# Filter loads of a spectral-mixer kernel: five ahead of the first weight transpose, four from GpSimd, the rest one to a row step

## Chip, cores and metric

The kernel runs on one core of a Trainium2 chip. The metric is the device time of one execution in microseconds; the median of several executions is compared. A core has five instruction streams that matter here: TensorE (PE in the profile, with its weight loads as PEld), VectorE (DVE), ScalarE (ACT), GpSimd (POOL) and SyncE (SP). SP computes nothing: it issues DMAs, in the order in which the program lists them, and an SP instruction that has to wait holds up all SP instructions after it. GpSimd can issue DMAs as well; they are a separate queue in the profile (q0, software_dynamic), while those of SP are q1 (hardware_dynamic).

## What is computed

The reference is the forward pass and all gradients of two residual blocks on x of 2048 x 448 in bf16:

```python
def _A_ref(x, w_r, w_i):
    X = rfft2(x.astype(float32)); X = X * (w_r + 1j * w_i)
    return irfft2(X, s=(S, D)).astype(bfloat16)
def _B_ref(x, w1, b1, w2, b2):
    h = _layernorm(x); u = gelu(einsum("bsd,sf->bdf", h, w1) + b1)
    return transpose(einsum("bdf,fs->bds", u, w2) + b2)
h  = x + _A_ref(_layernorm(x), w_r, w_i)
h2 = h + _B_ref(_layernorm(h), w1, b1, w2, b2)
# outputs: h2 and the gradients of sum(h2 * grad_out) by x, w_r, w_i, w1, b1, w2, b2
```

w_r and w_i, the spectral filter, are 2048 x 225 each. They are the tensors whose loads the change moves. w2 is 1792 x 2048.

## The kernel before, in words

The Fourier transforms are matrix products with tables that the kernel generates itself. The 2048 rows are 128 partitions times NT = 16 steps t. All four engine orders of PE, SP, DVE and ACT are written out by hand: an engine runs its instructions in the order of the Python program. GpSimd alone is ordered by a planner at build time. The part that matters here is the first 50 us of the run:

* **Start.** SP loads x, grad_out and four natural blocks of w2 (j = 0 to 3), which PE transposes itself (`turn_w2`). The other ten blocks of w2 (j = 4 to 13) come by transposing DMAs on SP, `load_w2T`, line 312. Five buffers go round: three in the region rE, two in rO.
* **Row steps** (`for t in range(NT)`, line 903). A step has a first product `row_a(t + 1)` for the next row group, with the folded input (`folds`, region rS, made on DVE by `fold_prep` or `fold_quarters`, one for two row groups) as stationary side and a scaled table `Rs[t + 1]` (region rX, `scale_R`, DVE) as moving side; then a second product `row_b(t - 3)`. Between them PE is filled with products of another matrix, w2 by grad_out (`dg_gen`, pulled by `fill(n)`). `scale_R(t + 3)` needs `rstd_x`, the inverse deviation of the layer norm. It is computed by Newton steps on GpSimd for two row groups at a time (`newton_gp`, lines 408 to 414), at the steps listed in `GROUPS`; the last group, rows 14 and 15, comes at t = 7.
* **Reshape.** When `row_b` has done two row groups and the result has left PSUM, a DMA on SP (line 687) lays it out for the next stage in D2. There are eight such DMAs; each is 226 KB.
* **Filter loads.** `w_io` (line 577) is a generator of 18 loads into rW: nine for w_r, nine for w_i. In each nine, numbers 0, 2, 4, 6 take 16 x 3600 elements (16 partitions), numbers 1, 3, 5, 7 take 16 x 16 x 225 (15 for number 1) in reversed order of rows, and number 8 takes 16 x 225. All are issued on SP. `W_AT` tells how many are drawn in step t: two in even steps and one in odd steps, t = 0 to 11.
* **Spectral stage** (`s2_stage`, line 690). It begins with products of 32 x 32 tables with D2 (lines 709 and 225, tile r as moving side), needs all of D2, and then multiplies by the filter on DVE (`fwd_mult`), which needs rW.

The first transposing DMA is issued at the head of step 0:

```python
    W_AT = {t: 1 if t % 2 else 2 for t in range(12)}
    for t in range(NT):
        if t == 0:
            load_w2T()
```

Of the kernel before, what the change touches and what calls it, by code (L numbers as in the profile page):

```python
# [103 lines left out]
class Ring:  # L104
# [7 lines left out]
    def next(self):  # L112
        v = self.views[self.i % len(self.views)]
        self.i += 1
        Ring.release(v)
        return v
# [8 lines left out]
def kernel(  # L125
# [20 lines left out]
    nc = tc.nc  # L146
# [4 lines left out]
    gp_ = nc.gpsimd  # L151
# [12 lines left out]
    def cut(reg, off, *dims):  # L164
        n = int(np.prod(dims))
        v = reg[:, off:off + n]
        if len(dims) == 1:
            return v
        names = "abcd"[:len(dims)]
        return v.rearrange("p (" + " ".join(names) + ") -> p " + " ".join(names),  # L170
                           **{c: d for c, d in zip(names, dims)})
# [131 lines left out]
    def load_w2T():  # L303
        j = w2T_ring.i
        if j == NFB:
            return
        wT = w2T_ring.next()
        w2Ts[j] = wT
        if j < N_NAT:
            nc.sync.dma_start(out=w2n[j], in_=B_w2[j * P:(j + 1) * P, :].rearrange("f (t c) -> f t c", c=P))  # L310
            return
        nc.sync.dma_start_transpose(out=wT, in_=B_w2[j * P:(j + 1) * P, :].rearrange("f (t c) -> f t c", c=P))
# [261 lines left out]
    Wc = cut(rW, 0, 2, NG, DF)  # L574
    W = Wc.rearrange("p c g k -> p g c k")

    def w_io(dr, di, store):
        Wq = Wc.rearrange("(q s) c g k -> s q c g k", s=2)
        for c_, d in ((0, dr), (1, di)):
            moves = []  # L580
            for i in range(4):
                moves.append((Wq[0][16 * i:16 * i + 16, c_].rearrange("l g k -> l (g k)"), 16 * i, [[P * DF, 16], [1, 16 * DF]]))
                g0 = 0 if i else 1
                moves.append((Wq[1][16 * i:16 * i + 16, c_, g0:NG, :], P - 16 * i - g0,
                              [[P * DF, 16], [-DF, NG - g0], [1, DF]]))
            moves.append((Wq[1][0:16, c_, 0, :], 64, [[P * DF, 16], [1, DF]]))
            for sb, row, dims in moves:
                d_ap = bass.AP(d.tensor, d.offset + row * DF, dims)
                nc.sync.dma_start(out=d_ap if store else sb, in_=sb if store else d_ap)
                yield  # L590

    r452_ring = ring(r452, 0, 8, 2, KW)
    Xs = cut(rX, 0, NG, 2, KW)
# [20 lines left out]
    def scale_R(t):  # L614
        v = Rs_ring.next()
        ve.tensor_scalar(out=v, in0=Rm[:], scalar1=rstd_x[:, t:t + 1], scalar2=None, op0=ALU.mult)
        return v
# [5 lines left out]
    def fold_prep(src, t2):  # L623
        ft = fold_ring.next()
        s0 = 2 * t2
        fv = ft[:, 0:2 * D].rearrange("p (s w j) -> p s w j", s=2, w=2)
        a = src[:, s0:s0 + 2, 0:D // 2]
        r = src[:, s0:s0 + 2, D - 1:D // 2 - 1:-1]
        ve.tensor_tensor(out=fv[:, :, 0, :], in0=a, in1=r, op=ALU.add)
        ve.tensor_tensor(out=fv[:, :, 1, :], in0=a, in1=r, op=ALU.subtract)  # L630
        folds[t2] = ft
# [5 lines left out]
    def fold_quarters(src, t2, i=None):  # L637
        ft = fold_ring.next()
        s0 = 2 * t2
        if i is None:  # L640
            i = m448.i % 8
            assert i % 2 == 0
            m448.next(), m448.next()
        pm = cut(r448, i * D, 2, 2, D // 2)
        fv = ft[:, 0:2 * D].rearrange("p (s k j) -> p s k j", s=2, k=4)
        a, b = src[:, s0:s0 + 2, 0:D // 2], src[:, s0:s0 + 2, D // 2:D]
        ve.tensor_tensor(out=pm[:, :, 0, :], in0=a, in1=b, op=ALU.add)
        ve.tensor_tensor(out=pm[:, :, 1, :], in0=a, in1=b, op=ALU.subtract)
        lo, hi = pm[:, :, :, 0:DC], pm[:, :, :, 2 * DC - 1:DC - 1:-1]
        ve.tensor_tensor(out=fv[:, :, 0:4:3, :], in0=lo, in1=hi, op=ALU.add)  # L650
        ve.tensor_tensor(out=fv[:, :, 2:0:-1, :], in0=lo, in1=hi, op=ALU.subtract)
        folds[t2] = ft

    def row_a(t, R):
        pa = ps_ff()
        ft = folds[t // 2]
        for k in range(4):
            o = DC * (4 * (t % 2) + k)
            mm(pa[:, k * P:(k + 1) * P], lhsT=ft[:, o:o + P], rhs=R, start=True, stop=True)
        if t % 4 == 0:  # L660
            blks[t // 4] = blk_ring.next()
        evac(out=blks[t // 4][:, :, t % 4, :], in_=pa[:].rearrange("p (n x) -> p n x", x=8))

    def row_b(h, quarters=None):
        u, e, c = h // 4, h // 2 % 2, h % 2
        if h < 0 or h >= NT:
            return
        pd = ps_ff()
        pv = pd[:, 0:452].rearrange("p (c k) -> p c k", c=2)
        pq = pd[:, 0:452].rearrange("p (c e k) -> p c e k", c=2, e=2)  # L670
        for w in (1, 0):
            for b in range(2):
                n = 4 * (4 * (2 * w + b) + 2 * c + e)
                lhsT = blks[u][0:DC, n:n + 4].rearrange("p i j x -> p (i j x)")
                if quarters is not None:
                    mm(pq[:, 1 - w, b, :], lhsT=lhsT, rhs=quarters[0:DC, w, b, 0:KW // 2], start=True, stop=True)
                    continue
                mm(pv[:, 1 - w, :], lhsT=lhsT, rhs=csF[0:DC, w, b, :], start=(b == 0), stop=(b == 1))
        if c == 0:
            css[h // 2] = cs_ring.next()  # L680
        cs = css[h // 2]
        if quarters is not None:
            evac(out=cs[:, c].rearrange("p w (j e) -> p w e j", e=2), in_=pq)
        else:
            evac(out=cs[:, c], in_=pv)
        if c:
            defer(RESH_LAG, lambda: resh[0].dma_start(out=D2[u:u + 125:4, 8 * e:8 * e + 8].rearrange("p g c k -> p (g c k)"),
                                                      in_=cs.rearrange("p x c k -> p (x c k)")), cs)
# [96 lines left out]
    def fill(n):  # L785
        while n > 0 and pending:
            try:
                next(pending[0])
                n -= 1
                if row_ops:  # L790
                    row_ops.pop(0)()
            except StopIteration:
                pending.pop(0)
# [5 lines left out]
    def ln_stats(src, t, mv):  # L799
        ve.bn_stats(out=stats[:, t, :], in_=src[:, t, :])  # L800
        if t % 2:
            ve.bn_aggr(out=mv[:, t - 1, :], in_=stats[:, t - 1, :])
        if t % 2:
            ve.bn_aggr(out=mv[:, t, :], in_=stats[:, t, :])
# [88 lines left out]
    GROUPS = {0: (6, 8), 1: (8, 10), 3: (10, 12), 5: (12, 14), 7: (14, 16)}  # L893
    STATS = {0: (6, 7), 1: (8, 9), **{t: (t + 8,) for t in range(2, 8)}}
    INV_S = {10: 0, 11: 1, 12: 2, 13: 3}
    W_AT = {t: 1 if t % 2 else 2 for t in range(12)}
    for c in range(2):
        for e in range(2):
            sc.copy(out=Rp.rearrange("p (e a q b c) -> p c e a q b", e=2, c=2, q=8, a=2)[:, c, e],
                    in_=Rm[:, 64 * c + 32 * e:64 * c + 32 * e + 32].rearrange("p (q a b) -> p a q b", q=8, a=2))  # L900
    FILL_A = (4, 4, 8, 12, 6, 3, 3, 3, 3, 3, 3, 3, 3, 3, 3, 3)
    FILL_B = (0, 0, 2, 2, 2, 2, 4, 4, 3, 2, 2, 2, 2, 2, 2, 2)
    for t in range(NT):
        if t == 0:
            load_w2T()
        if t + 1 < NT:
            row_a(t + 1, Rs.pop(t + 1))
        fill(FILL_A[t])
        if 1 <= t and t + 3 < NT:
            if t + 3 in (4, 8, 12):  # L910
                while Meter.side:
                    Meter.side.pop(0)()
            Rs[t + 3] = scale_R(t + 3)
        row_b(t - 3, csQ if t - 3 >= 4 * U_Q else None)
        if t == NT - 1:
            for i in range(t - 2, NT):
                row_b(i, csQ)
        if t % 2 and t < 12:
            if t // 2 + 2 < 2 * U_Q:
                fold_prep(xn, t // 2 + 2)  # L920
            else:
                fold_quarters(xn, t // 2 + 2, t // 2 % 2 * 2)
        if t == 4:
            for w in range(2):
                gp_.tensor_copy(out=csQ[:, w, :, :], in_=csF[:, w, 0, :].rearrange("p (j e) -> p e j", e=2))
        if t == 1:
            sc.activation(out=warm, in_=half_r, func=ACT.Sin, scale=1.0 / 64.0)
            while cs_ops:
                cs_ops.pop(0)()
        for i in STATS.get(t, ()):  # L930
            ln_stats(xn, i, mvx)
        for _ in range(3 if t > 0 else 0):
            if next(uv, None):
                break
        if t in GROUPS:
            a, b = GROUPS[t]
            newton_gp(mvx[:, a:b, 1], rstd_x[:, a:b], slice(a, b))
        for _ in range(W_AT.get(t, 0)):
            next(w_loads, None)
        if t in INV_S:  # L940
            gen_inv_s(INV_S[t])
        if t == 2:
            gen_RT()
        fill(FILL_B[t])
# [500 lines left out]
```

## Time and profile before

| what | value |
|---|---|
| median of 3 runs | 342.64 us (342.21 to 345.09) |
| the profiled execution, its own time | 343.32 us |
| its span, first to last instruction | 341.5 us |
| PE busy | 330.4 us, 97% |
| DVE, ACT, POOL busy | 251.5, 205.2, 82.8 us |
| granted TensorE clock | 1.000 |
| DMA, share of 16 engines: q1 (SP) and q0 (POOL) | 86.7% and 4.9% |

Times in the views are microseconds from the start of the span. Each line of a timeline gives start, duration, engine, line of the code, operation, out<-in, shape, number of instructions merged, and in brackets the idle time of the engine before it with what ended it. A "q" after the engine's name (SPq) marks an instruction that is issued but keeps no arithmetic busy; the duration of an SP DMA is the time to issue it, and the time until its data has landed is listed apart. Tiles without a name of their own are shown as r.

### The profile page before, as it was taken

To read this page: it belongs to the slowest core of one execution; us is meant where nothing else is said; L and a number is where in the kernel's file an instruction comes from. 1 tells how busy PE (TensorE), PEld (TensorE's weight loads), DVE (VectorE), ACT (ScalarE), POOL (GpSimd) and SP (SyncE) were. 2 spreads that over 40 slices of the span, in tenths; PEclk is the share of its full clock that TensorE was granted. 3 is DMA by queue.
4 is the path that set the end of the run, shared out by engine and by line. 5 is a ranking of instruction groups with operands and counts; after the bars stand their busy time and mean duration, and the time that the engine had idled before them with its cause. 6 is when DMAs were issued, how large, how long until landed. Compare 5 with 4: busy or idle time off the path is not lost.

```text
span 341.5 us, 7952 instructions
## 1 busy us (share of the span) xinstructions
PE 330.4 (97%) x2877; PEld 173.5 (51%) x2877; DVE 251.5 (74%) x672; ACT 205.2 (60%) x447; POOL 82.8 (24%) x253
## 2 busy tenths in 40 slices
PE   8899979999999999999999999999999999999995
PEld 4565644456645555555555555554333334555552
DVE  8999438834967888594225988787589984499994
ACT  5886746856966553513222345566478875688882
POOL 7756102451320000001001111120002222156650
PEclk9999999999999999999999999999999999999999
DMA  7998999977999999967976999848998999999975
GB/s 271 396 157 179 194 247 165 198 153 228 252 286 326 330 321 236 222 200 226 207 169 144 177 180 190 159 110 169 236 302 256 232 238 314 273 193 298 230 272 206
DMA packets 137966, 78.03 MB, mean 228 GB/s; under 512 B 88712, under 2 KB 129416, under 8 KB 137800
## 3 DMA queue, kind: packets, MB, share of 16 engines
q1 hardware_dynamic: 135368, 73.82, 86.7%
q0 software_dynamic: 2560, 3.72, 4.9%
q8 instruction: 22, 0.36, 0.5%
q14 instruction: 16, 0.13, 0.1%
HBM read 27.81 MB, written 22.04 MB: 146 GB/s over the span
## 4 chain that ended last, share of the span: by engine, by line
PE 71%; DVE 1%; ACT 1%; issue 0%
PE ps_mm L220 63%; PE ps_ff L220 6%; PE ps_ff L225 2%; ACT rO L84 1%; DVE rA L84 1%; DVE rB L84 0%; ACT rAT L84 0%; ACT rC L84 0%; DVE rG L84 0%; ACT rstd_h L84 0%; DVE rstd_h L84 0%
## 5 line engine op out<-in xcount | busy, mean ns | idle before, releaser
L220 PEld LDWEIGHTS <-r 128*128 128x128 bf16 (+2 forms) x628 | 58.6, 105 | 47.2 <-issue 2.5
L220 PEld LDWEIGHTS <-rS 128*128 128x128 bf16 (+1 forms) x468 | 36.3, 97 | 32.9 <-issue 6.4
L84 ACT CAST rO<-ps_mm 128x512 bf16<-128x512 f32 (+1 forms) x69 | 36.8, 584 | 14.4 <-PE ps_mm L220 13.0
L220 PE MATMUL ps_mm<-rD,r 128*128 128x448 bf16 x224 | 44.5, 352 | 0.0
L220 PEld LDWEIGHTS <-rst 128*128 128x128 bf16 (+1 forms) x320 | 23.6, 97 | 31.3 <-issue 14.0
L724 POOL DMA_DIRECT2D r<-r x32 | 19.2, 606 | 68.8 <-ACT r L84 61.6
L220 PE MATMUL ps_mm<-rC,rE 128*128 128x448 bf16 x144 | 32.1, 353 | 0.6 <-issue 0.6
L220 PE MATMUL ps_mm<-rB,r 128*128 128x448 bf16 x160 | 31.2, 353 | 0.1
L220 PE MATMUL ps_mm<-rG,rst 128*128 128x512 bf16 (+1 forms) x128 | 28.7, 380 | 0.2 <-ACT rO L84 0.2
L220 PE MATMUL ps_mm<-r,rst 128*128 128x512 bf16 (+2 forms) x144 | 27.4, 345 | 0.0
L84 ACT CAST r<-ps_ff 128x452 bf16<-128x452 f32 x44 | 23.7, 587 | 5.8 <-PE ps_ff L225 3.8
L84 ACT ACTIVATE r<-ps_mm,rstd_h 128x448 bf16<-128x448 f32 x16 | 10.1, 634 | 26.8 <-PE ps_mm L220 26.8
L84 DVE SCALAR_TENSOR_TENSOR r<-ps_mm,b2col,r 128x448 bf16<-128x448 f32 x16 | 10.9, 683 | 19.9 <-PE ps_mm L220 18.2
L84 ACT ACTIVATE r<-rC 128x448 bf16<-128x448 bf16 x16 | 9.1, 571 | 26.7 <-DMA out_dram<-r 22.4
L1182 POOL TENSOR_SCALAR lcol<-lcol 128x1 f32<-128x1 f32 x16 | 8.5, 530 | 64.7 <-ACT r L84 64.7
L84 ACT ACTIVATE rG<-rG 128x896 bf16<-128x896 bf16 x14 | 13.3, 950 | 14.9 <-DVE rG L84 14.7
L220 PEld LDWEIGHTS <-rO 128*128 128x128 bf16 (+1 forms) x165 | 15.4, 98 | 12.3 <-ACT rO L84 0.2
L84 ACT CAST rS<-ps_ff 128x512 bf16<-128x512 f32 x32 | 18.7, 589 | 2.5 <-PE ps_ff L220 2.4
L220 PE MATMUL ps_ff<-csI,rAT 113*128 113x224 bf16 (+1 forms) x108 | 19.0, 298 | 0.6 <-ACT rAT L84 0.4
L84 DVE TENSOR_SCALAR rG<-rG 128x896 bf16<-128x896 bf16 x28 | 10.9, 389 | 10.0 <-ACT rG L84 10.0
L220 PE MATMUL ps_mm<-rC,rO 128*128 128x448 bf16 x80 | 18.1, 353 | 0.0
L84 ACT CAST rG<-ps_mm 128x512 bf16<-128x512 f32 (+1 forms) x28 | 13.8, 534 | 6.8 <-PE ps_mm L220 6.7
(199 smaller groups left out, 633.8 us busy)
## 6 DMA issues: line engine op xcount, KB each, us to landing
out_dram<-rO SPq DMA_DIRECT2D x34, 256.0 KB, 2.8
r<-in_B_w_dram SPq DMA_DIRECT2D x5, 1024.0 KB, 8.9
r<-r POOLq DMA_DIRECT2D x32, 113.0 KB, 5.7
out_dram<-rG SPq DMA_DIRECT2D x11, 256.0 KB, 2.3
r<-r SPq DMA_DIRECT2D x12, 226.0 KB, 3.3
r<-in_B_w_dram SPq DMA_DIRECT2D x3, 896.0 KB, 5.4
rS<-in_B_w_dram SPq DMA_DIRECT2D x3, 896.0 KB, 5.8
rB<-in_B_w_dram SPq DMA_DIRECT2D x4, 512.0 KB, 7.6
```

The lines of the kernel that those rows point to most:

```text
L84: fn(**kw)
L220: nc.tensor.matmul(out, lhsT=lhsT, rhs=rhs, start=start, stop=stop)
L225: nc.tensor.matmul(out, lhsT=lhsT, rhs=rhs, start=start, stop=stop)
L724: defer(RESH_LAG, lambda g=g, ab=ab: gp_.dma_start(out=D3[rowbase(g):rowbase(g) + 29:4, :, :, :], in_=ab), ab)
L1182: gp_.tensor_scalar(out=m1, in0=ms, scalar1=-1.0 / D, scalar2=None, op0=ALU.mult)
```

## The change

Three things change in the schedule of the 18 filter loads and of the first transposing load. First, `W_AT` becomes 3 in step 0, 2 in step 1, one each in steps 2 to 5 and 8 to 12, and the first `load_w2T()` moves from the head of step 0 to step 1, behind the loads of that step. Second, of the nine loads of w_i, numbers 0, 2, 4 and 6 are issued by GpSimd, and they are not counted as a draw: number 0 is issued with number 1, and so on. Third, before the first load of w_i a memset on DVE writes one element per partition of rW's w_i half.

```diff
             moves.append((Wq[1][0:16, c_, 0, :], 64, [[P * DF, 16], [1, DF]]))
-            for sb, row, dims in moves:
+            if not store and c_:
+                nc.vector.memset(Wc[:, 1, 0, 0:1], 0.0)
+            for n, (sb, row, dims) in enumerate(moves):
                 d_ap = bass.AP(d.tensor, d.offset + row * DF, dims)
-                nc.sync.dma_start(out=d_ap if store else sb, in_=sb if store else d_ap)
-                yield
+                eng = gp_ if not store and c_ and n in (0, 2, 4, 6) else nc.sync
+                eng.dma_start(out=d_ap if store else sb, in_=sb if store else d_ap)
+                if eng is nc.sync:
+                    yield
...
-    W_AT = {t: 1 if t % 2 else 2 for t in range(12)}
+    W_AT = {0: 3, 1: 2, **{t: 1 for t in (2, 3, 4, 5, 8, 9, 10, 11, 12)}}
...
     for t in range(NT):
-        if t == 0:
-            load_w2T()
         if t + 1 < NT:
             row_a(t + 1, Rs.pop(t + 1))
...
         for _ in range(W_AT.get(t, 0)):
             next(w_loads, None)
+        if t == 1:
+            load_w2T()
```

In the built program the orders of PE and ACT are the same as before. DVE has one instruction more, the memset, between `scale_R(11)` and `scale_R(12)`; the build gives it a wait for four of the w_r loads, those of the numbers 1, 3, 5 and 7. SP has four DMAs fewer. The planner puts the four DMAs of GpSimd one after the other into the Newton steps of row groups 14 and 15, behind line 409 and ahead of the first instruction of line 411; the first of them waits for DVE's memset.

## The prediction

> **What bounds the kernel now.** I read the engine table first, then PE's waits, then the timelines of SP, PE, POOL and DVE over the first 50 us.
>
> ```profile
> PE 330.4 (97%) x2877; PEld 173.5 (51%) x2877; DVE 251.5 (74%) x672; ACT 205.2 (60%) x447; POOL 82.8 (24%) x253
> ```
>
> PE is busy 330.4 of 341.5 us. A change that leaves PE's instructions as they are can win only a piece of PE's 11 idle us. PE's waits, longest first:
>
> ```profile
> PE ps_ff L225 <- DMA r<-rX: 2.4, 1, 2.4
> PE ps_ff L220 <- DVE rS L84: 1.3, 2, 0.7
> PE ps_mm L375 <- DVE rS L621: 1.2, 1, 1.2
> ```
>
> One wait is larger than the others: 2.4 us, once, at the start of the spectral stage, for a reshape DMA out of rX. PE's timeline has the place, and SP's timeline what is ahead of that DMA:
>
> ```profile
> 50.03 0.77 PE L225 MATMUL ps_ff<-r,Vt 32*32 32x452 bf16 x16 [2.37 <-DMA r<-rX]
> ```
>
> ```profile
> 13.59 5.80 SPq L312 DMA_TRANSPOSE rO<-in_B_w_dram  x1
> 19.44 3.31 SPq L589 DMA_DIRECT2D rW<-in_A_w_r_dram  x5
> 22.86 5.56 SPq L312 DMA_TRANSPOSE rE<-in_B_w_dram  x2
> 28.48 1.93 SPq L589 DMA_DIRECT2D rW<-in_A_w_r_dram  x3
> ...
> 42.86 1.91 SPq L589 DMA_DIRECT2D rW<-in_A_w_i_dram  x3
> 44.88 0.58 SPq L687 DMA_DIRECT2D r<-r  x1
> 45.50 0.60 SPq L589 DMA_DIRECT2D rW<-in_A_w_i_dram  x1
> 46.20 2.57 SPq L687 DMA_DIRECT2D r<-rX  x4
> ```
>
> From 13.59 to 48.77 each SP instruction begins within 0.1 us of the end of the one before it: SP does nothing but issue. The last four reshapes go out from 46.20, though the last of their data left PSUM at 43.9 (ACT, rX). So SP's issue time sets the end here, and PE, ready at 50.03 - 2.37 = 47.66, waits for it.
>
> **What goes from SP.** Four loads of w_i leave SP ahead of the last reshape. Three take 1.91 and one has to wait its turn, so 0.64 us each: 4 x 0.64 = 2.6 us. The last reshape would land at 50.03 - 2.6 = 47.4, before PE comes at 47.66. The gain, by this alone, is the whole stall: 2.37 us. What is late next is PE itself.
>
> **Five loads ahead of the first transpose.** The transpose is moved past five loads on SP. SP holds eight DMAs in flight here: each waits for the eighth before it. The transpose had the place of 13.59; the five loads now wait for the start-up loads one by one. By the landings of those start-up loads (4096- and 3584-byte rows, issued at 8.62 and 9.38, landed 18.3 and 19.6) the fifth goes out between 18.4 and 19.6, and the transpose between 19.0 and 20.2. It took 5.80 when it stood in the full queue, and 2.10 to 3.33 later, so I take 2.8: SP is through with the six at 21.8 to 23.0, against 22.75 before. I take 0.6 us ahead, bounds 1.5 ahead and 3.3 behind (20.2 + 5.80). The transposed block (j = 4) is first used by PE at 29.6; the transpose at 13.59 landed after 7.7 us, so at the latest 27.9. It costs nothing, covered by 1.7 us; without that cover PE would wait by the difference.
>
> **The memset.** It is one DVE instruction of about 0.06 us (the memset at 0.80 is that short), but it waits for w_r loads 1, 3, 5 and 7. Load 7 is the 26th SP instruction, as before, when it went out at 29.79 and landed 4.5 us later, at 34.3. With SP 0.6 ahead: 33.7. DVE comes to it at 32.3 (after the first of the two rX at 32.09). So DVE stands for 1.4 us. Behind it on DVE are `scale_R(12)`, the fold for row groups 12 and 13, and `scale_R(13)`; PE waits for that fold with `row_a(12)` at 34.77. The fold ended at 33.82, a slack of 0.9, so PE would stand 0.5 us here. It does not add to the next item, which sets a later time for the same PE order.
>
> **The four DMAs on GpSimd.** This is the item that decides. They stand in the middle of the Newton steps for rows 14 and 15:
>
> ```profile
> 33.74 0.19 POOL L409 TENSOR_SCALAR rstd_x<-mvx 128x2 int32<-128x2 int32 x1
> 34.02 0.19 POOL L411 TENSOR_TENSOR nt_f<-rstd_x 128x2 f32<-128x2 f32 x1
> ...
> 35.95 0.19 POOL L414 TENSOR_TENSOR rstd_x<-nt_f,rstd_x 128x2 f32<-128x2 f32 x1
> ...
> 58.00 2.63 POOL L724 DMA_DIRECT2D r<-r  x4 [14.29 <-ACT r L84]
> 63.04 2.36 POOL L724 DMA_DIRECT2D r<-r  x4 [2.42 <-ACT r L84]
> ```
>
> ```profile
> 36.18 0.32 DVE L84 TENSOR_SCALAR rX<-Rm,rstd_x 128x128 bf16<-128x128 bf16 x1 [0.17 <-POOL rstd_x L414]
> 36.40 0.68 DVE L84 TENSOR_TENSOR r<-rA 128x448 bf16<-128x448 bf16 x2
> 37.12 0.69 DVE L84 TENSOR_TENSOR rS<-r 128x448 bf16<-128x448 bf16 x2
> ...
> 38.33 0.39 PE L220 MATMUL ps_ff<-rX,rS 128*128 128x128 bf16 x4
> ```
>
> The chain: Newton ends 36.14, DVE already waits for it (0.17), scales the table for row 14 at 36.18, folds rows 14 and 15 until 37.81, and PE takes the fold in `row_a(14)` at 38.33. From DVE's end to a waiting PE it takes 0.06 elsewhere (27.14 to 27.20), so the slack is 38.33 - 37.81 - 0.06 = 0.46 us. Four issues on POOL cost 2.63 after a long pause, 2.36 otherwise. The trace has none with rows of 7200 bytes on POOL. From below I bound an issue by a small POOL operation, 0.23 (L984 at 81.40), 0.9 for four; from above by 2.63, and by the longest POOL row here, 0.91, for each of four, 3.6. I take 2.63, the row that is nearest. PE then stands at `row_a(14)` for 2.63 - 0.46 = 2.17 us, if the memset is done when POOL arrives at 33.93 (33.7, so just).
>
> The DVE instructions of those 2.6 us run beside the DMAs or wait for Newton. POOL's issues at 58.00 took 0.60 to 0.84 each with DVE at 900-element products. The Trainium skill (SBUF — State Buffer, the box on DVE blocking DMA in its part on the doors to the memory) says that a GpSimd DMA of some 620 ns takes some 3100 ns beside a DVE copy that locks the shared port. By that page four would be an estimated 12.4 us and PE's stall 11.9. The trace shows no case of it, and DVE is idle in most of that window.
>
> **The sum.** PE comes to the spectral stage at 47.66 + 2.17 = 49.83. The last rows leave PSUM 2.17 later, at 46.0, their reshape needs 2.4 to land: 48.4, so no wait remains. The stage starts at 49.83 instead of 50.03: 0.2 us won. From there PE is gapless but for 0.6, 0.4 and two 0.2 us in the next 40 us, so the shift is carried to the end. The profiled span would be 341.3 and its own time 343.1; that execution stood 0.7 over the median, so the forecast for the median is 342.64 - 0.2 = 342.4 us. In short: the stall of 2.37 at the stage's head is exchanged for one of 2.17 twelve us earlier.
>
> **Rivals.**
>
> *POOL's issue is cheap.* 16 rows of 7200 bytes may cost less than a line-724 DMA (2560 packets of q0 by 32 issues: 80 each). At 0.9 for four, PE stands 0.44 and the stage starts at 48.1, which the reshape (47.4) allows: 1.9 won, 340.7. With the whole stall gone 340.3. For it: the rows are a fifth of that. Against it: SP pays 0.6 for 16 rows and for 240 alike, and POOL's 0.60 is the same in 15 of 16 issues at 58 to 75 us.
>
> *The memset holds everything (slower).* If load 7 lands later than 34.1, POOL's first DMA starts with it, and each us later is a us later at `row_a(14)`. At 34.1 the change is worth nothing; at 35.6 it loses 1.5: 344.1; with the transpose at its old 5.80, load 7 lands at 37.6: 3.5 lost, 346.1. For it: load 7 landed at 34.3 before, already over that point, and three transposes now stand close together ahead of it, each 512 KB. Against it: the first transpose meets an emptier queue.
>
> *SP isn't freed.* Two transposes with only one reshape between them could take back what the four loads gave (2.10 and 3.33 now): the reshape then lands at 50 and PE waits again, 342.9.
>
> *POOL's issue is dear.* At 0.91 each PE stands 3.2 at `row_a(14)`: 343.4. For it: the first issue at 58.00 took 0.84. Against it: none of the others did.
>
> **How the numbers follow.** Forecast 342.4 (341.8 to 343.0): 0.46. Cheap POOL issue (340.3 to 341.8): 0.25. Late memset (343.0 to 346.1): 0.19. SP not freed: 0.05. Dear POOL issue: 0.05. The range, 340.3 to 344.8, leaves out the end of the late memset (0.07), of the dear issue (0.03) and a little below. One per cent, 3.4 us, is about what this measurement can tell from nothing. Faster by more needs more than the whole stall: 0.03. Slower by more is the end of the late memset, 0.05, and an issue dearer than any row, 0.02. Within: 0.90.
>
> **What would show it.** PE's wait for the DMA from rX should be gone or under 0.3 us. A new PE wait of about 2.2 us should stand at a `ps_ff` product of rX and rS, ended by DVE rS, near 38 to 41 us. POOL should show four DMAs of rW at 34 us, and Newton's last line 414 at 38.8. The memset on DVE should start between 32.3 and 34.8, released by a DMA. SP should begin its last four reshapes when their data is there, not when it is free. Wrong would be: no stall at `row_a(14)` (then POOL's issue is cheap), or the stage's head still waiting for SP.

## The result and the profile after

The changed kernel is slower: 349.15 us in the median (four executions, 345.79 to 349.92) against 342.85 for the kernel before beside it, a ratio of 1.0138 (95% interval 1.0090 to 1.0187). Single executions of both kernels scatter by some microseconds, in part since the granted clock falls to half for a few microseconds in some of them; those with a mean granted clock of 0.997 or more are called executions at full clock. Of the changed kernel's four executions, which were its only ones, three lie below that (0.995, 0.990 and 0.989); the one at full clock took 345.79, which suggests that a part of the 6.3 us between the medians is the clock's. Small differences are read below from landmarks in the profiles, and a part of the cause of the scatter is among the findings.

The profiled execution of the changed kernel took 348.78 us, with a span of 346.8. The engine table of its page:

```profile
PE 331.4 (96%) x2868; PEld 173.9 (50%) x2877; DVE 251.5 (73%) x673; ACT 205.2 (59%) x447; POOL 85.6 (25%) x257
```

PE has the same work, and 15.4 us without any instead of 11.1. The longest of PE's waits (total, times, longest):

```profile
PE ps_ff L220 <- DVE rS L84: 3.4, 3, 1.8
PE ps_ff L225 <- DMA r<-rX: 2.5, 1, 2.5
```

The wait that was to go is still there, with 2.5 us instead of 2.4. Two new ones have come, for the fold. PE's timeline has all three, and one line more that matters:

```profile
37.01 0.40 PE L220 MATMUL ps_ff<-rX,rS 128*128 128x128 bf16 x4 [1.83 <-DVE rS L84]
...
41.78 0.40 PE L220 MATMUL ps_ff<-rX,rS 128*128 128x128 bf16 x4 [1.03 <-DVE rS L84]
...
53.62 0.81 PE L225 MATMUL ps_ff<-r,Vt 32*32 32x452 bf16 x16 [2.50 <-DMA r<-rX]
...
58.69 0.41 PE L225 MATMUL ps_ff<-r,Vt 32*32 32x452 bf16 x16
```

The first line is `row_a(12)`, the second `row_a(14)`, the third the head of the spectral stage, the fourth the stage's second group. The same four in the profile before stood at 34.77, 38.33, 50.03 and 53.79. So the loss builds up in steps:

| landmark | before | after | later by | step |
|---|---|---|---|---|
| `row_a(11)` | 32.80 | 33.04 | 0.24 | 0.24 |
| `row_a(12)` | 34.77 | 37.01 | 2.24 | 2.00 |
| `row_a(14)` | 38.33 | 41.78 | 3.45 | 1.21 |
| PE ready for the spectral stage | 47.66 | 51.12 | 3.46 | 0.01 |
| the stage's first product | 50.03 | 53.62 | 3.59 | 0.13 |
| its second group | 53.79 | 58.69 | 4.90 | 1.31 |
| end of the span | 341.5 | 346.8 | 5.3 | 0.4 |

DVE's timeline shows what is behind the first two steps, and POOL's timeline the rest of it:

```profile
35.30 0.06 DVE L588 MEMSET rW<- 128x1 bf16 x1 [2.72 <-DMA rW<-in_A_w_r_dram]
...
40.08 0.32 DVE L84 TENSOR_SCALAR rX<-Rm,rstd_x 128x128 bf16<-128x128 bf16 x1 [1.83 <-POOL rstd_x L414]
```

```profile
35.66 2.23 POOL L592 DMA_DIRECT2D rW<-in_A_w_i_dram  x4 [2.20 <-DVE rW L588]
...
39.85 0.20 POOL L414 TENSOR_TENSOR rstd_x<-nt_f,rstd_x 128x2 f32<-128x2 f32 x1
```

DVE stands for 2.72 us ahead of the memset, for a load of w_r. POOL stands 2.20 for the memset, then issues four DMAs in 2.23, and the last Newton step ends at 40.05 instead of 36.14, 3.91 later. `row_a(14)` follows 1.73 behind that end, at 41.78; before it could have come at 36.14 + 1.73 = 37.87, and PE came at 38.33, with 0.46 to spare. 3.91 - 0.46 = 3.45 is the whole delay of `row_a(14)`: GpSimd sets it, and the stall at `row_a(12)` is a part of it, not an addition. SP's timeline:

```profile
13.83 7.95 SPq L592 DMA_DIRECT2D rW<-in_A_w_r_dram  x5
21.82 2.71 SPq L312 DMA_TRANSPOSE rO<-in_B_w_dram  x1
...
36.20 3.83 SPq L312 DMA_TRANSPOSE rO<-in_B_w_dram  x1
40.13 0.61 SPq L592 DMA_DIRECT2D rW<-in_A_w_i_dram  x1
40.83 0.58 SPq L691 DMA_DIRECT2D r<-r  x1
41.46 2.08 SPq L592 DMA_DIRECT2D rW<-in_A_w_i_dram  x2
43.64 0.91 SPq L691 DMA_DIRECT2D r<-r  x1
44.60 2.47 SPq L592 DMA_DIRECT2D rW<-in_A_w_i_dram  x2
48.06 2.72 SPq L691 DMA_DIRECT2D r<-rX  x4
```

SP has four DMAs fewer to issue, and is later: the last four reshapes begin at 48.06 instead of 46.20. Five loads of w_i take 0.61, 2.08 and 2.47 where two took 1.25 before; the first reshape comes out at 48.06, just behind 48.00, where the transposing load issued at 36.20 has landed. That load (block j = 8 of w2) is the eighth DMA of SP before this reshape, and SP holds eight in flight. The next two reshapes as well go out only when the eighth DMA before each has landed (out at 48.79 and 49.57, the landings at 48.71 and 49.50), so it is not block 8 alone that is late but what was issued behind it too. The table of DMA issues between 36 and 48 us gives the time from issue to landing, the last number of each line. Before:

```profile
r<-r SPq DMA_DIRECT2D x3, 226.0 KB, 3.3
...
rO<-in_B_w_dram SPq DMA_TRANSPOSE x1, 5.4
```

After:

```profile
r<-r SPq DMA_DIRECT2D x3, 226.0 KB, 8.2
rW<-in_A_w_i_dram POOLq DMA_DIRECT2D x4, 112.5 KB, 7.5
...
rO<-in_B_w_dram SPq DMA_TRANSPOSE x1, 11.8
```

The transposing load needs 11.8 us instead of 5.4, and the three reshapes in this stretch 8.2 instead of 3.3, beside GpSimd's four loads. The experiments ask whether this is cause and effect, which part of the change carries which step, and where the 1.31 us behind the stage's head come from.

### The profile page after: what moved, and what is told of

Its sections match the earlier page's. It is cut to its first block, busy times and chain, and to the rows that moved or that the text cites. A ratio compares the mean times of both kernels' runs of the same rounds, so it can differ in the third digit from the quotient of the medians.

```text
span 346.8 us, 7953 instructions
## 1 busy us (share of the span) xinstructions
PE 331.4 (96%) x2868; PEld 173.9 (50%) x2877; DVE 251.5 (73%) x673; ACT 205.2 (59%) x447; POOL 85.6 (25%) x257
## 4 chain that ended last, share of the span: by engine, by line
PE 73%; ACT 3%; issue 1%; DVE 1%; POOL 0%; ACTq 0%
PE ps_mm L220 65%; PE ps_ff L220 6%; PE ps_ff L225 2%; ACT rO L84 2%; DVE rA L84 1%; ACT rAT L84 0%; ACT rX L84 0%; DVE rB L84 0%; ACT rD L84 0%; ACT rC L84 0%; DVE rG L84 0%; ACT rstd_h L84 0%; POOL nmean_h L988 0%; DVE rstd_h L84 0%; ACTq L84 0%
## 5 line engine op out<-in xcount | busy, mean ns | idle before, releaser
L220 PE MATMUL ps_mm<-rC,rE 128*128 128x448 bf16 x144 | 32.9, 359 | 0.8 <-issue 0.8
L220 PE MATMUL ps_mm<-rG,rst 128*128 128x512 bf16 (+1 forms) x121 | 26.9, 380 | 1.0 <-issue 0.8
L220 PEld LDWEIGHTS <-rE 128*128 128x128 bf16 x144 | 12.8, 98 | 10.3 <-issue 1.9
```

The costliest lines, as they stand in the source:

```text
L220: nc.tensor.matmul(out, lhsT=lhsT, rhs=rhs, start=start, stop=stop)
```

## Experiments

The texts of the expectations name one theory and several rivals. Theory 1: the GpSimd loads with their memset carry the loss, by the row steps and by the transposing load of block 8. Rival 2: the new order at the head carries it. Rival 3: the head waits for SP or the DMAs whatever is done on GpSimd. Rival 4: the clock falls by history or chance. Rival 5: the reshapes are slow by themselves. The kernel before was run beside each group of experiments; its medians there were 346.31 (19 executions), 344.64 (29), 343.95 (29) and 344.51 (17).

### Which part carries which step

**The new head alone.** All 18 loads on SP in the new order of the head; no memset, nothing on GpSimd.

```diff
-            if not store and c_:
-                nc.vector.memset(Wc[:, 1, 0, 0:1], 0.0)
...
-                eng = gp_ if not store and c_ and n in (0, 2, 4, 6) else nc.sync
+                eng = nc.sync
...
-    W_AT = {0: 3, 1: 2, **{t: 1 for t in (2, 3, 4, 5, 8, 9, 10, 11, 12)}}
+    W_AT = {0: 3, 1: 2, **{t: 1 for t in (2, 3, 4, 5, 12)}, **{t: 2 for t in (8, 9, 10, 11)}}
```

> All 18 filter loads on SP, no memset; five loads ahead of the first transpose as in the changed kernel, and each load that GpSimd took goes back to SP at the same row step. Theory 1 (GpSimd's four DMAs and the memset carry the loss): the two new PE stalls at row_a(12) and row_a(14) are gone; SP stays about 0.9 us behind the kernel before, since the fourth load waits for the start-up loads until 20.1 us; the stage's head begins at about 51 us, stall 3.3 us; time 0.9 to 1.3 us over the kernel before if the clock stays full, some 1.5 more if it halves after that stall. Rival 2 (the five loads ahead of the transpose carry it): time within 2 us of the changed kernel, 347 us or more, with PE at full clock.

Measured: 344.59 us in the median, ratio 1.0024 (0.9972 to 1.0075). Its six executions at full clock have a median of 344.19, the eight of the kernel before beside it 343.02. No stall in the row steps; block 8 lands in 5.8 us; but the stage's head waits:

```profile
52.26 0.97 PE L225 MATMUL ps_ff<-r,Vt 32*32 32x452 bf16 x16 [4.47 <-DMA r<-rX]
```

With the same 18 loads on SP, the new head makes this wait 4.47 instead of 2.37: the last four reshapes begin at 48.39, 2.2 us later than in the kernel before. The five loads do not use SP's time better; they wait for the start-up loads. And with nothing on GpSimd block 8 is as fast as before.

**The memset cut by partitions.** Rows 0 to 95 are cleared at load 0, rows 96 to 127 only ahead of load 6, so that GpSimd's first three loads wait for nothing late. By the same edit the fourth comes later, behind the Newton steps.

```diff
-            if not store and c_:
-                nc.vector.memset(Wc[:, 1, 0, 0:1], 0.0)
...
+                if not store and c_ and n in (0, 6):
+                    nc.vector.memset(Wc[0:96, 1, 0, 0:1] if n == 0 else Wc[96:128, 1, 0, 0:1], 0.0)
```

> The changed kernel with the memset split: partitions 0 to 95 ahead of load 0 of w_i, partitions 96 to 127 ahead of load 6, three row steps later. The first then waits for w_r loads 1, 3 and 5 only, not for load 7; GpSimd's fourth DMA moves behind the Newton steps. Theory 1: DVE does not stand, row_a(12) has no stall (2.0 us less); three DMAs of 1.75 us in all delay Newton, row_a(14) stands 1.3 us; the transposing load of block 8 still lands late (45 us or more), so the stage's head keeps a stall, and begins between 50.5 and 52.5; time 1 to 3 us below the changed kernel, more if the clock stays full. Rival 3 (the stage's head is bound by SP and DMA alone, and the row stalls are hidden in that wait): the head begins within 0.5 us of 53.6 and the time does not move.

Measured: 343.85 us, ratio 1.0018 (0.9987 to 1.0049): the loss is no longer to be told from the scatter. The memset runs at 33.01, GpSimd issues three loads from 34.38 and the fourth at 40.37, and `row_a(12)` has no stall:

```profile
40.02 0.40 PE L220 MATMUL ps_ff<-rX,rS 128*128 128x128 bf16 x4 [0.79 <-DVE rS L84]
...
50.06 0.62 PE L225 MATMUL ps_ff<-r,Vt 32*32 32x452 bf16 x16 [0.71 <-DMA r<-rX]
```

```profile
rO<-in_B_w_dram SPq DMA_TRANSPOSE x1, 8.2
```

So the late memset carries most of the 1.4%. Against the changed kernel `row_a(14)` comes 1.76 earlier (40.02 for 41.78), the head waits 1.79 less, and no half clock follows at the head (1.31, see below): 4.9 us together, where the spans differ by 4.7. That the head gains because fewer of GpSimd's loads fall into the landing time of block 8 is argued here from its 8.2 us; the thin rows below test it.

**The old head, with memset and GpSimd loads.**

```diff
-    W_AT = {0: 3, 1: 2, **{t: 1 for t in (2, 3, 4, 5, 8, 9, 10, 11, 12)}}
+    W_AT = {**{t: 2 - t % 2 for t in range(6)}, **{t: 1 for t in range(8, 13)}}
...
+        if t == 0:
+            load_w2T()
...
-        if t == 1:
-            load_w2T()
```

> The changed kernel with the head of before for w_r: the first transposing load first, then two and one loads of w_r by turns; memset and GpSimd loads stay as changed. Theory 1 (GpSimd loads and memset carry the loss): load 7 goes out at about 29.8 and lands at 34.3 as before, so DVE stands until 34.4, PE stands 0.9 at row_a(12), GpSimd's DMAs start at 34.8, row_a(14) stands about 1, the transposing load of block 8 needs over 8 us beside them, and the stage head waits again; 345 to 349 us. Rival 2 (the new head order carries it): 342 to 343 us, no stall at row_a(12).

Measured: 346.53 us, ratio 1.0076 (1.0036 to 1.0115). Neither theory's numbers: load 7 landed earlier than I expected, the memset ran at 32.83 and `row_a(12)` did not stall; what was left is 1.12 at `row_a(14)`, 9.6 us for block 8 and 1.15 at the head. So the GpSimd loads cost something even with the memset in time. And the new head makes load 7 late: it landed at 34.3, 32.6 and 34.3 in three other profiles with the old head (the kernel before, and before with block 8's load or the last four loads behind), and at 35.1 and 35.2 in two with the new one (the head alone, and the thin rows). DVE comes to the memset at some 32.6 us, so what the memset costs differs from execution to execution.

### What slows the transposing load

**GpSimd's rows cut to 450 bytes.** As many DMAs and rows on GpSimd, a sixteenth of the bytes; the whole rows are loaded by SP behind the last reshape, so that the total (354.36 us) says nothing.

```diff
+                if eng is gp_:
+                    late.append((sb, d_ap))
+                    d_ap = bass.AP(d.tensor, d.offset + row * DF, [[P * DF, 16], [1, DF]])
+                    sb = sb[:, 0:DF]
...
+    for o, i_ in late:
+        nc.sync.dma_start(out=o, in_=i_)
```

> The changed kernel with the four GpSimd loads cut from rows of 7200 bytes to rows of 450 bytes, 16 rows each as before; the whole rows are loaded by SP behind the last reshape, so that its total time is not to be compared, only the stretch up to the stage head. Theory 1 (it is the bytes of GpSimd's rows that crowd the transposing load): the memset and the four issues stay where they are (0.5 to 0.7 us each, PE stands about 1.8 at row_a(12) and 1.0 at row_a(14)), but the transposing load of block 8 lands in 5.5 to 8 us instead of 11.8, and the stage head waits under 0.7. Rival (the queue or the issue itself, not the bytes): 10 us or more, and a wait of about 2.5 us.

The table of DMA issues of this kernel, again between 36 and 48 us:

```profile
r<-rX SPq DMA_DIRECT2D x4, 226.0 KB, 2.5
...
rW<-in_A_w_i_dram POOLq DMA_DIRECT2D x4, 7.0 KB, 4.0
rO<-in_B_w_dram SPq DMA_TRANSPOSE x1, 5.5
```

Memset (35.30), GpSimd's four issues (35.67 to 37.90) and the two stalls in the row steps (1.43 and 1.03) are where they were; block 8 lands in 5.5 us, and the head, at 51.05, does not wait at all. It is the bytes of GpSimd's rows that slow the transposing load, not the issues and not the queue. The 2.50 us at the head of the changed kernel are the price of that.

**Block 8's load behind the reshapes.** One transposing load fewer goes out ahead of the spectral stage.

```diff
-CAP = 9
+CAP = 8
```

> The changed kernel with CAP = 8 instead of 9: the transposing load of block 8 (issued at 36.2, landed at 48.0 us in the changed kernel) goes behind the last reshape on SP. Theory 1 (that load, slowed by GpSimd's 7200-byte packets, holds SP and the reshapes): SP is free at 42 us, the last reshape goes out when its data is there (47.3), the stage's head begins at 51.2 without a stall, the clock stays full; 2.4 us plus 1.3 us less in the span: median 345 to 346 us. Rival 5 (the reshapes are slow by themselves while GpSimd's DMAs run): the head still waits 1.5 us or more.

Measured: 346.07 us from four executions, ratio 1.0117 (0.9999 to 1.0235), too wide to tell; the profiled one took 343.42, with a span of 341.4. In it the two row stalls stand (1.63 and 1.03), the stage starts at 50.59 with no wait, and GpSimd's rows land in 4.3 us instead of 7.5. So the two transfers slow each other, and with one moved away the wait at the head is gone.

**GpSimd's loads later.** The old head, and the loads of w_i drawn from step 11 on, so that memset and GpSimd DMAs are behind the last Newton step.

```diff
-    W_AT = {0: 3, 1: 2, **{t: 1 for t in (2, 3, 4, 5, 8, 9, 10, 11, 12)}}
+    W_AT = {**{t: 2 - t % 2 for t in range(6)}, 11: 2, 12: 1, 13: 1, 14: 1}
...
+        if t == 0:
+            load_w2T()
...
-        if t == 1:
-            load_w2T()
```

> The changed kernel with the head of before and the loads of w_i drawn from step 11 on, so that memset and GpSimd's four DMAs stand behind the last Newton step. Theory 1 (the place of the GpSimd loads costs, not GpSimd): no stall at row_a(12) and row_a(14), the four DMAs at 36.5 to 39.5, the transposing load of block 8 still slow (8 to 11 us) but PE does not need it before 49; SP issues its last four reshapes from 45 on, a wait at the stage head of at most 0.7, its start at 47.7 to 48.4; about 341.3 us in executions at full clock (340.8 to 342.2). Rival (GpSimd's rows slow the transposing load, and this alone holds SP): a wait of 1.5 us or more at the head, 342.6 or more.

Measured: 345.24 us, ratio 1.0044 (1.0020 to 1.0068). The rival's numbers came, but not by its mechanism. There is no stall in the row steps, and block 8 (out at 35.34) landed in 4.7 us, at 40.05, before the first of GpSimd's rows had landed (44.96); SP was not held by it. But now these rows (39.0 to 47.8) are in the air with the reshapes. The table of issues between 36 and 48 us:

```profile
r<-rX SPq DMA_DIRECT2D x4, 226.0 KB, 6.4
...
rW<-in_A_w_i_dram POOLq DMA_DIRECT2D x4, 112.5 KB, 6.6
```

The reshapes land in 6.4 us where the profile before has 2.4, and the head waits 2.21. At both places tried, something that is due there pays for the four loads.

### Is SP's issue time what sets the head, and can it be won?

**The kernel before, with block 8's load behind the reshapes** (`CAP = 8` alone).

> The kernel before with one transposing load fewer ahead of the spectral stage: that of block 8 goes out behind the last reshape; nothing else changes. If that transposing load is what holds the reshapes on SP: SP reaches the last reshape about 3.3 us earlier, PE's wait at the stage head falls from 2.37 to under 0.3, the stage starts at 47.7 to 48.0, no half clock follows, and the time is about 340.3 us (339.8 to 341.2). Rival 5 (the reshapes wait for their data or for DMA bandwidth, not for SP): the wait stays at 1.5 us or more and the time within 1 us of before.

Measured: 344.69 us, ratio 0.9986 (0.9949 to 1.0024). The stage starts at 47.76, with no wait, and the reshapes from rX land in 2.6 us, no faster than the 2.4 before: SP was what the head waited for, not the transfers. But PE's timeline shows the next thing that is late:

```profile
51.65 3.73 PE L220 MATMUL ps_mm<-rC,rO 128*128 128x448 bf16 x10 [2.25 <-DMA rO<-in_B_w_dram]
```

PE would use block 8 from 49.4 on, and now waits for it.

**The changed kernel with both repairs**, the cut memset and `CAP = 8`.

> The changed kernel with both repairs: the memset cut by partitions, so that GpSimd's first three loads wait for no late load of w_r, and block 8's transposing load behind the reshapes. Theory 1: no stall at row_a(12), at most 0.8 us at row_a(14), no wait at the stage head, which starts at 48.5 to 49.4; about 341.5 us (340.8 to 342.6), no half clock. Against the kernel before with the second repair alone (the run beside it) it should be 0.8 to 1.5 us slower, since GpSimd's loads then relieve an SP that is no longer late and only their stall is left. Rival 2 (the head order carries a loss of its own): 343 us or more.

Measured: 345.98 us, ratio 1.0011 (0.9969 to 1.0053). Head at 48.69, no wait, 0.81 at `row_a(14)`; and 1.63 for block 8 at 51.96. The numbers at the head came as expected, the time did not: in part for the same reason, and in part by a stall of 3.5 us near 68 us, which is told in the last section.

**The kernel before, with the last four loads of w_i behind the last reshape.** SP is freed of the same 2.6 us that the change meant to free, and GpSimd is left alone.

```diff
-    W_AT = {t: 1 if t % 2 else 2 for t in range(12)}
+    W_AT = {**{t: 1 if t % 2 else 2 for t in range(8)}, 8: 1, 9: 1}
...
+    flush()
     for _ in w_loads:
         pass
```

> The kernel before with the last four loads of w_i on SP behind the last reshape instead of ahead of it; nothing on GpSimd, no memset. It takes the same 4 x 0.64 = 2.6 us from SP ahead of the reshape as the change meant to. If SP's issue time sets the stage head: no wait there (under 0.4), start at 47.7 to 48.1, the four loads land by 51, DVE's first products with the filter wait for them by up to 1.5 us and PE by at most 0.5; 341.0 us in executions at full clock (340.6 to 341.8). Rival (the filter is needed too early): a new PE wait of 1 to 2 us in the stage's first inverse rows, 342 to 343 us.

Measured: 343.63 us, ratio 0.9984 (0.9947 to 1.0022). Head at 48.31, no wait. The rest of the gain goes back at the filter's first use:

```profile
56.13 0.38 PE L225 MATMUL ps_ff<-rS,UVT 32*32 32x452 bf16 x16 [1.49 <-DVE rS L84]
```

DVE's first product with the filter waited 1.55 us for the last of the moved loads, and PE 1.49 for DVE.

**The same with two loads behind** (`8: 2, 9: 1, 10: 1` in `W_AT`).

> The kernel before with the last two loads of w_i on SP behind the last reshape instead of the last four. With four behind, the wait at the stage head (2.37) went, but DVE's first product with the filter waited 1.55 for the last loads and PE 1.49 for that. With two behind, SP is freed of 1.28 us ahead of the reshape: the wait at the head should be 0.8 to 1.2 us, the start at 48.6 to 49.2, the two loads should land by 51.6, DVE should wait under 0.4 and PE under 0.4 more; about 1.2 us less than before in executions at full clock (341.6 to 342.4). By the clock theory no wait is long enough to bring a half window at the head, so that the share of executions with a mean clock below 0.997 falls under a quarter. If instead the two waits trade one for one: the time of before, and of four behind.

Measured: 343.72 us, ratio 0.9979 (0.9943 to 1.0016). The head waits 1.49 in the profiled execution, more than expected; DVE and PE do not wait for the filter. One of 12 executions had a mean clock below 0.997, as against 7 of 17 of the kernel before beside it. So the share below full clock fell, as expected. No version beats the kernel before by more than the measurement can tell.

### Where the 1.31 us behind the head come from

From the first product of the stage to its second group the changed kernel takes 5.07 us, the kernel before 3.76. The windows of the changed kernel's profile (busy PE, PEld, DVE, ACT, POOL, then the granted clock):

```profile
33.31:36.72 3.41, 1.86 (x44) 0.92 (x40) 1.38 (x6) 1.48 (x4) 1.21 (x3) 1.00 0.76 145
36.72:40.13 3.41, 3.12 (x88) 2.17 (x88) 1.07 (x4) 2.21 (x5) 2.78 (x13) 1.00 1.19 210
50.37:53.78 3.41, 0.91 (x16) 0.36 (x14) 0.67 (x2) 0.00 (x0) 0.00 (x0) 1.00 1.02 263
53.78:57.20 3.42, 3.42 (x55) 1.68 (x48) 0.73 (x2) 1.85 (x4) 0.00 (x0) 0.50 1.16 166
57.20:60.61 3.41, 3.41 (x63) 1.68 (x61) 3.24 (x8) 1.21 (x3) 0.00 (x0) 1.00 0.90 200
```

The clock is 0.50 for exactly 3.41 us behind the stall. The kernel before, whose stall was as long, has no such window:

```profile
45.72:49.13 3.41, 1.94 (x11) 0.78 (x8) 1.36 (x5) 0.47 (x2) 0.00 (x0) 1.00 0.91 274
49.13:52.55 3.42, 2.52 (x56) 1.49 (x57) 0.55 (x2) 1.53 (x4) 0.00 (x0) 1.00 0.98 218
```

The difference is where the stall lies on a grid. In the trace's record of the clock, the half stretch of the changed kernel begins 47.79 us after the clock first rose to full (6.00), which is 14 times 3.413; the kernel before rose at 4.76, and 13 such steps later, at 49.13, a step boundary cuts its stall of 2.37 into 1.47 and 0.89. PE stood 2.50 of 3.41 us in the window ahead of the half one, and in no window of the kernel before more than 1.47.

**Products without use in the gap of the changed kernel.** 14 of them between the row steps and the stage.

```diff
+    bridge = ps_mm()
+    for _ in range(14):
+        nc.tensor.matmul(bridge[:, 0:D], lhsT=ident[:], rhs=xn[:, 0, :], start=True, stop=True)
```

> The changed kernel plus 14 products of 128x448 on PE into a spare PSUM buffer just ahead of the spectral stage, 2.6 us of work in the place of the 2.5 us of idle time; their result is used by nothing. Theory 1 (PE's clock is halved because PE stood idle there): clock 1.000 through 50 to 60 us, the products after the stall at their old duration, 1.3 us less in the span, median near 346 us. Rival 4 (the clock is halved for what went before, or by chance): clock under 1 again and the time within 0.7 us of the changed kernel.

Measured: 347.0 us from four executions, ratio 1.0113 (1.0052 to 1.0174). There is no half window at 54 us, but one at another place, behind the 1.63 us stall of `row_a(12)`, which fell into one window here:

```profile
34.11:37.52 3.41, 1.78 (x45) 1.02 (x44) 1.77 (x7) 1.18 (x3) 1.67 (x3) 1.00 1.06 201
37.52:40.94 3.42, 3.42 (x48) 1.94 (x46) 1.30 (x4) 1.72 (x4) 2.38 (x12) 0.50 0.96 170
```

**The same in the kernel before.**

> The kernel before with 14 products without use (ident by row group 0, 128x448 each, about 2.7 us) between PE's last product of the row steps and the spectral stage: PE works where it stood 2.37 us; nothing else changes. Clock theory (the granted clock is set in windows of about 3.4 us on a grid that each execution starts elsewhere, and a window is at half speed when PE stood for over about 1.6 us of the window ahead of it): no half window in the profile before the end, the mean clock of nearly all executions at 0.997 or more, where about half of those of before lie below that, and a time close to the full-speed executions of before, 343 to 343.6 us, with few over 344.5. Rival 4 (the clock falls by itself): as many executions below 0.997 as before has, and the same median.

Measured: 345.2 us, ratio 1.0039 (1.0000 to 1.0077). The clock did as expected: 2 of 12 executions below a mean of 0.997, against 13 of 29 of the kernel before beside it. The time did not: the ten others spread over 343.25 to 345.51. So the half window is not all of the scatter.

Over all fourteen profiles, at full clock: where PE stood 1.63 us or more of a window (1.63, 2.02, 2.25, 2.41, 2.49, 2.50 and 3.41), the next one was at half; where it stood 1.55 or less (1.55, 1.54, 1.49, 1.47, 1.44 and below), it was at full. Rival 4 holds only so far as the start of the grid is chance. What stays open: if the stall is 2.37 and the bound about 1.6, and if each execution starts anywhere on the grid, the kernel before should escape in 2 x 1.6 - 2.37 = 0.8 of 3.41 us, a quarter of its executions; 51 of its 94 had a mean clock of 0.997 or more. Its stall must often be shorter than in the profiled execution, or the bound isn't the same everywhere.

## Why the prediction was wrong

The forecast was 342.4 us in a range of 340.3 to 344.8; the median is 349.15, and the one execution at full clock, 345.79, lies outside as well. The forecast span was 341.3, the measured one 346.8. PE was to be at the stage's head at 49.83 with no wait left; it was there at 51.12 and waited 2.50 more. So of the 5.5 us, 1.29 are from the row steps, 2.50 from a wait that was to be gone, 1.31 from the clock, and 0.4 from the rest of the run.

* **"What goes from SP": this step failed.** The four DMAs left SP, but not their time. The working took the other DMAs' durations from the trace before, although the change puts the same bytes on the same DMA engines from a second queue at the same time. Block 8 then lands in 11.8 us instead of 5.4, SP's eighth place is taken until 48.00, and the reshapes start 1.86 later, where SP's issue time alone would have had them 2.6 earlier. With the bytes cut, the wait is gone. "What is late next is PE itself" failed too: with SP freed in other ways, the next to be late was block 8 (2.25) or the filter (1.49). That SP's issue time sets the stage's head was right: the head stood at 47.76 without a wait once SP was freed of one transposing load.
* **"Five loads ahead of the first transpose": wrong in sign, inside its bounds.** SP was to be through with the six between 21.8 and 23.0; it was at 24.53. The fourth and the fifth load waited for the two start-up loads whose landings I had read as 18.3 and 19.6; with the new order these landed at 20.12 and 21.23 (out at 20.14 and 21.25). It is the same step once more: a landing taken from the trace before that came later in the new one. So SP was behind by 1.8 there, and by 1.0 at load 7 (30.75 against 29.79).
* **"The memset": the mechanism was right, the size off.** Load 7 (the 27th DMA of SP in both kernels, not the 26th) was to land at 33.7 and DVE to stand for 1.4; the memset ran at 35.30 behind 2.72, and PE stood 1.83 at `row_a(12)`. "It does not add to the next item" holds for that stall, which is inside the 3.45 of `row_a(14)`, but not for the memset: load 7 beyond 34.1 makes GpSimd's issues late by as much. The rival "the memset holds everything" has this place, this point and this price: its 35.30 - 34.1 = 1.2 on top of the forecast 49.83 gives PE ready at 51.0; measured 51.12. That they agree to 0.1 is partly luck, since the issues took 0.4 less than was taken and PE was 0.24 late before `row_a(12)`. It was given 0.19, and it assumed, as the forecast did, that the wait at the head would be gone.
* **"The four DMAs on GpSimd": right.** They stand in the Newton steps, behind line 409. Their issue took 2.23 (0.74, 0.53, 0.48, 0.48) where 2.63 was taken and 0.9 to 3.6 bounded. With the memset in time (the old head) Newton ended 2.18 later than before, at 38.32, and `row_a(14)` came 1.71 later, at 40.04: the slack of 0.46 was read rightly, and the item was worth 1.71 where 2.17 was taken. PE's stall there was only 1.12 because PE itself came 0.59 later. The Trainium skill (SBUF — State Buffer, the section A bandwidth-pool intuition that's wrong) gives some 3100 ns for one GpSimd DMA beside a DVE copy; here the four issues took 0.48 to 0.74 each, the first two beside DVE's folds (35.53 to 36.95). The folds are not such a copy, so no run here tries that case.
* **"SP isn't freed" was the outcome, by another cause.** Its 0.05 was for two transposing loads with one reshape between them. What took the time back was contention with GpSimd's rows; in the run with the new head alone the two transposing loads stand as close (34.57 and 37.27, with one reshape between), and block 8 takes 5.8.
* **"The sum" had no term for the clock.** It carried the shift at the stage's head unchanged to the end; 1.31 us came on top behind the head, from 3.41 us at half speed.

By landmarks, then: 2.00 at `row_a(12)` and 1.21 at `row_a(14)`, together what Newton's late end costs, 0.13 for a wait that should have given back 2.37, 1.31 for the clock, and 0.6 spread over the start and the end make the 5.3 us of the two spans. The chances were wrong for one reason above all: neither the forecast nor a rival priced a DMA that takes longer to land than before.

## What to carry to other kernels

To move a load from one queue to another takes away its issue, not its bytes: look at what is in the air at its new time, and at what on the old queue waits for that. An instruction that stands in for a wait (here a memset that waits for four loads) is priced by the last load to land and by everything behind it on two engines; a finer region may be most of the repair, as the cut by partitions was here. And a stall of 1.6 us or more on PE can be paid twice, in the stall and in the half clock behind it, if it falls into one step of the clock's grid.

## What the runs showed of the hardware

* **The clock is granted in steps of 3.413 us on a grid that starts elsewhere in each execution.** In the fourteen profiles it first rises to full between 3.87 and 7.05 us, and the stretches between its changes are whole numbers of steps (47.787 us is 14, 30.720 is 9, 6.827 is 2). A step is at half speed when PE stood for about half of the one before it (1.63 us did it, 1.55 did not). The Trainium skill (TensorE: Matmul & The Clock Gate, the section Why this matters for your kernels) asks for no gaps over some 3 us; here gaps of 1.63 to 2.50 us were enough where they lay in one step, so the measurement differs from the page. A step can also follow at half speed when PE stood for less while already at half (0.91 us in the run with GpSimd's loads later, 1.44 in that with the thin rows).
* **GpSimd's rows of 7200 bytes and a transposing load slow each other**: 11.8 and 7.5 us together; 5.5 us for the transposing load beside rows of 450 bytes, and 4.3 for the rows without it.
* **A second place scatters.** Some 67 to 68 us into the run PE stands for a time with no releaser: 0.6 in the profile before, 1.9 in that with two loads behind, 2.9 in that with GpSimd's loads later, and most in that with both repairs (PE's waits there between 46 and 80 us; total, times, longest):

```profile
PE ps_mm L220 <- issue: 3.5, 1, 3.5
```

In each of the four an instruction packet of 16 KB ends 1.4 to 1.6 us ahead of PE's return; it starts at 65.9, 66.6, 68.4 and 68.7 in this order. That PE waits for this packet is argued from the order alone; what the packet holds is not shown, and nothing was tried on it.
